# Attention by clusters with token mixing on one core: maxima over half the keys in single PSUM banks, weighted sums in runs of three units

## The chip, the cores and the metric

The kernel runs on one core of one Trainium2 chip. The metric is device time in microseconds (us), lower is better. TensorE multiplies matrices and writes PSUM, which has eight banks of 512 fp32 columns; VectorE (DVE in the profile), ScalarE (ACT), GpSimd (POOL) and SyncE (SP, which issues DMAs) work beside it. Each engine takes its instructions in order and waits for the others by semaphores.

## The reference

There are 4 batches, 8 heads, 768 positions, 64 columns to a head and 16 clusters. Attention goes only between a query and the keys of the same cluster; a token mixing layer follows. Cut to what matters:

```python
q_assign = np.argmax(np.einsum('bhsd,hcd->bhsc', q_n, c_n), axis=-1)
k_assign = np.argmax(np.einsum('bhsd,hcd->bhsc', k_n, c_n), axis=-1)
mask = q_assign[:, :, :, None] == k_assign[:, :, None, :]
scores = scale * np.matmul(q, k.transpose(0, 1, 3, 2))
scores = np.where(mask, scores, -1000000000.0)
scores = scores - np.max(scores, axis=-1, keepdims=True)
attn = np.exp(scores)
attn = attn / (np.sum(attn, axis=-1, keepdims=True) + 1e-09)
x = np.matmul(attn, v)          # heads side by side: 4 x 768 x 512
theta = x @ w_theta
y = w_tok_r @ (x * np.cos(theta)) + w_tok_i @ (x * np.sin(theta))
u = x + y
out = u + np.maximum(u @ w_ch, 0.0)
```

## The kernel before

Two heads of one batch make a **pair**; there are 16 pairs, and the two heads of one lie in partitions 0 to 63 and 64 to 127. The keys of a pair are cut into six tiles of 128 and the queries into two halves `a` of 384, so a pair has 12 **units** (`NU`), one for each half and tile of keys `i`, and the attention part has 192 (`NUT`).

In unit `u` the program issues, in this order:

- `scores(u)` (L335): four products for both heads, eight matmuls with 64 rows each into two PSUM banks of the pool `ps` (tiles `sc`). The last of the four, `mk` by `mq`, adds the mask and the negative row maximum. ScalarE takes the exponentials into a tile `at` (six buffers), and POOL adds them up by threes into `acc`.
- `row_max(u + LEAD)` (L304), in odd units only: the maxima of a tile of 128 queries over all 768 keys. Eight matmuls fill two tiles `m` of two banks each, one for each head, from the pool `ps0`, whose two buffers are four banks; then VectorE reduces 768 columns at a time into `nm`, with the sign turned.
- `weighted` (L387), in even units, for two units at a time, three and four units behind the scores: `at` by the values `vt`, matmuls with 128 rows, into the one bank `av`.
- whatever the table `todo` holds for that unit: the small pieces.

The small pieces of TensorE are `lg` (products with the cluster centres), `lt` (their transposes), `ot` (transposes of the one-hot assignments, twice a pair), `mt` (transpose of the maxima in `shift_row`, twice a pair) and `sm` (column sums of `acc` in `sums`). Behind `lt` VectorE finds the cluster of each query and key in steps of their own units: `mxl` and `eq` (L244, L246), the product with `wc` and the maximum `rr` (L250, L252), and `ohp` (L254). `A_UNITS`, `HI_UNITS`, `LO_UNITS`, `SUMS` and `NORM` say in which unit each step of a pair stands; a pair is prepared two pairs, 24 units, ahead of its scores. `shift_row` sends the transposed maxima by ScalarE and two DMAs into a row of `mq`, where `scores` reads them.

Besides, 14 blocks of weights are turned from 64-bit to 32-bit numbers and split. Block `x` starts at unit 13x; it has two VectorE instructions at 13x+4 (L128, L130, behind a ScalarE instruction, L127), two at 13x+8 (L133, L135), and a ScalarE copy and a POOL subtraction at 13x+11.

The order within an engine is fixed: `in_order` ties each instruction to the one in front of it on its engine, in the order in which the program issues them. A step that waits therefore holds up all that stands behind it on its engine. Tiles of a pool go round its buffers in turn, and a new tile waits until the old one's readers are done. Ahead of unit 0, the units from -LEAD on hold only maxima, pieces of the first pairs and two filling matmuls each (`WARM`). After the last unit the PSUM pools are closed and the token mixing part follows; its order is left to the scheduler, and the change does not touch it.

Of the kernel before, what the change touches and what calls it, by code (L numbers as in the profile page):

```python
# [9 lines left out]
F32 = mybir.dt.float32  # L10
# [4 lines left out]
ALU = mybir.AluOpType  # L15
AX = mybir.AxisListType
PSUM = bass.MemoryType.PSUM

BIG = float(2.0 ** 60)
N_M = 2  # L20
N_AV = 1
LEAD = 11
PW = 256
TAIL = 2
WARM = 2
SUMS = (5, 6, 8, 10, 12)
NORM = (14, 16)
TERMS = 3
EARLY = 3
LAG = 3  # L30
NAT = 6
AHEAD = 2
INV_2PI = float(1.0 / (2.0 * math.pi))
# [8 lines left out]
def kernel(  # L42
# [19 lines left out]
    nc = tc.nc  # L62
    B, H, D, S = qT.shape
    P = 128
    NP = H // 2
    NT = S // P
# [3 lines left out]
    HS = S // 2  # L70
# [7 lines left out]
    identf = cpool.tile([P, P], F32, name="identf")  # L78
# [83 lines left out]
    actx = ExitStack()  # L162

    ps0 = actx.enter_context(tc.tile_pool(name="ps0", bufs=N_M, space=PSUM))
    ps = actx.enter_context(tc.tile_pool(name="ps", bufs=8 - 2 * N_M - N_AV, space=PSUM))
    ps_av = actx.enter_context(tc.tile_pool(name="ps_av", bufs=N_AV, space=PSUM))
    pe = actx.enter_context(tc.tile_pool(name="pe", bufs=1))
    NPAIR = B * NP
# [1 line left out]
    for x in range(3):  # L170
        x = (NPAIR + x) % 3
# [4 lines left out]
    p2 = actx.enter_context(tc.tile_pool(name="p2", bufs=2))  # L176
    p1 = actx.enter_context(tc.tile_pool(name="p1", bufs=1))

    def bank(name, pool=None):
        return (pool or ps).tile([P, 512], F32, tag="bank", name=name)  # L180
# [28 lines left out]
    def f(ap):  # L209
        return ap.bitcast(F32)  # L210
# [78 lines left out]
    NH = NT // 2  # L289

    def split_u(u):
        pi, x = divmod(u, NU)
        return (pi,) + divmod(x, NT)

    def heads(*products):

        for n, (outs, stat, cols, mov, over) in enumerate(products):
            for j in range(2):
                r = slice(64 * j, 64 * j + 64)
                nc.tensor.matmul(  # L300
                    outs[j], lhsT=stat[r, cols], rhs=mov[r, over],
                    start=(n == 0), stop=(n == len(products) - 1))

    def row_max(u):  # L304


        pi, a, i = split_u(u)
        s = st[pi]
        if i == 0:
            s["nm", a] = p2.tile([P, 2, NH], F32, tag="nm", name=f"nm{u}")  # L310
        t = a * NH + i // 2
        m = [ps0.tile([P, 2, 512], F32, tag="m", name=f"m{u}_{j}") for j in range(2)]
        q = slice(t * P, (t + 1) * P)
        for c in range(2):
            k = slice(c * HS, (c + 1) * HS)
            outs = [m[j][:, c, 0:HS] for j in range(2)]
            heads((outs, s["hq"], q, s["hk"], k), (outs, s["mq"], q, s["mk"], k))
        for j in range(2):
            nc.vector.tensor_reduce(  # L319
                out=s["nm", a][:, j, i // 2:i // 2 + 1], in_=m[j][:, :, 0:HS], op=ALU.max, axis=AX.XY,  # L320
                negate=True)

    def shift_row(pi, a):

        s = st[pi]
        mt = bank(f"mt{pi}{a}")[0:NT, 0:P]
        nc.tensor.transpose(out=mt, in_=s["nm", a].rearrange("p j t -> p (j t)"), identity=identf)
        mr = p2.tile([NT, P], F32R, tag="mr", name=f"mr{pi}{a}")
        nc.scalar.copy(out=mr, in_=mt)
        for j in range(2):  # L330
            nc.sync.dma_start(
                out=f(s["mq"][64 * j + 32:64 * j + 33, a * HS:(a + 1) * HS]).rearrange("o (t n) -> o t n", n=P),
                in_=f(mr[j * NH:(j + 1) * NH]))
# [18 lines left out]
    def sums(pi):  # L352

        s = st[pi]
        sm = bank(f"sm{pi}")[:, 0:HS]
        for x in range(NT // TERMS):
            for j in range(2):
                for a in range(2):
                    g = 2 * j + a
                    nc.tensor.matmul(  # L360
                        sm[32 * g:32 * g + 32], lhsT=ecol, rhs=s["acc", a, x][:, j],
                        start=(x == 0), stop=(x == NT // TERMS - 1))
        se = p2.tile([P, HS], F32, tag="se", name=f"se{pi}", bufs=1)

        if pi < NPAIR - 1:
            nc.scalar.activation(out=se, in_=sm, func=AF.Identity, bias=eps)
        else:
            last_sum[0] = nc.vector.tensor_scalar_add(se, sm, 1e-9)
        yield

        sd = [dram.tile([4, HS], F32, tag=f"sd{x}", name=f"sd{x}{pi}", bufs=2) for x in range(2)]
        over = [x.rearrange("g (r n) -> (g r) n", r=32) for x in sd]
        nc.sync.dma_start(out=sd[0], in_=se.rearrange("(g r) n -> g r n", r=32)[:, 0])
        yield
        sq = p2.tile([P, 4 * HS // P], F32, tag="sq", name=f"sq{pi}")
        nc.sync.dma_start(out=sq, in_=over[0])
        yield
        nc.vector.reciprocal(out=sq, in_=sq)
        nc.sync.dma_start(out=over[1], in_=sq)
        yield  # L380
        s["rb"] = p1.tile([P, 2, HS], F32, tag="rb", name=f"rb{pi}")
        for j in range(2):
            last_load[0] = nc.sync.dma_start(
                out=s["rb"][64 * j:64 * j + 64],
                in_=sd[1][2 * j:2 * j + 2].unsqueeze(0).broadcast_to([64, 2, HS]))

    def weighted(u):  # L387
        pi, a, i = split_u(u)
        s = st[pi]
        if i == 0:  # L390
            s["av"] = ps_av.tile([P, 512], F32, tag="av", name=f"av{u}")[:, 0:HS]
        for j in range(2):
            nc.tensor.matmul(  # L393
                s["av"][64 * j:64 * j + 64], lhsT=s["vt"][:, i, j, :], rhs=s["at", a, i][:, j],
                start=(i == 0), stop=(i == NT - 1))
        if i == NT - 1:
            if a == 0:
                s["xt"] = p2.tile([P, 2, HS], F32, tag="xt", name=f"xt{pi}")
            nc.scalar.copy(out=s["xt"][:, a], in_=s["av"])

    def normalise(pi):
        b, p = divmod(pi, NP)
        s = st.pop(pi)

        (nc.gpsimd if pi < NPAIR - 2 else nc.vector).tensor_tensor(
            out=s["xt"], in0=s["xt"], in1=s["rb"], op=ALU.mult)
        yield
        nc.sync.dma_start(out=xT_d[b][:, p], in_=s["xt"].rearrange("p a s -> p (a s)"))
# [14 lines left out]
    NUT = NPAIR * NU  # L423
    todo = {}

    def at_unit(u, fn, *a):
        todo.setdefault(u, []).append((fn, a))

    def stages(units, gen):

        for u in units:
            at_unit(u, lambda: next(gen, None))
        at_unit(units[-1] + 1, run, gen)
# [15 lines left out]
                tail[ins.engine] = ins.name  # L449


    A_UNITS = (-2, 1, 3, 4, 6, 9, 11)
    HI_UNITS = dict(q=0, k=2)
    LO_UNITS = dict(q=2, k=4)
    W_UNITS = (4, 8, 11)
    W_EVERY = 13
    def prepare(pi, gen):
        u = NU * (pi - 2)
        stages([u + k for k in A_UNITS[1 if pi == 1 else 0:]], gen)
        for n in "qk":  # L460
            at_unit(u + HI_UNITS[n], part_hi, pi, n)
            at_unit(u + LO_UNITS[n], part_lo, pi, n, nc.gpsimd)

# [13 lines left out]
    for pi in range(NPAIR):  # L477
        u = NU * pi
        if pi > 0:
            prepare(pi, g1 if pi == 1 else assign(pi))  # L480
            at_unit(u - NU + 7, load_v, pi)
        for a in range(2):
            at_unit(u + a * NT - LEAD + NT, shift_row, pi, a)
        stages([u + NU + k for k in SUMS], sums(pi))
        stages([u + NU + k for k in NORM], normalise(pi))
    for x, gen in enumerate(early_weights()):
        u = W_EVERY * x
# [2 lines left out]

    idle = ps_av.tile([P, 512], F32, tag="av", name="idle")
    u = -LEAD
    while u < NUT + LAG or todo:
        start = len(nc.cur_bb.bb.instructions)
        if 0 <= u < NUT:
            scores(u)
        if u % 2 and u + LEAD < NUT:
            row_max(u + LEAD)
        for _ in range(WARM if u < 0 else 0):
            nc.tensor.matmul(idle[:, 0:P], lhsT=identb, rhs=identb, start=True, stop=True)  # L500
        if (u - LAG) % 2 and 0 <= u - LAG < NUT:
            weighted(u - LAG - 1)
            weighted(u - LAG)
        for x in sorted(x for x in todo if x <= u):
            for fn, a in todo.pop(x):
                fn(*a)
        in_order(start)
        u += 1
# [209 lines left out]
    u = None  # L718
    for part in range(S // PW):
# [4 lines left out]
        u = add_y(B - 1, part * PW, (part + 1) * PW)  # L724
# [53 lines left out]
```

## Time and profile before

| | us |
|---|---|
| median of 3 runs (lowest, highest) | 861.87 (858.85, 863.61) |
| the profiled execution, its own time | 864.6 |
| its span, first to last instruction | 862.8 |
| TensorE busy | 824.7 (96%) |
| VectorE busy | 466.8 (54%) |
| ScalarE busy | 402.5 (47%) |
| POOL busy | 470.6 (55%) |

Busy time of TensorE is modelled at the ends of its matmuls, and two matmuls that run side by side on 64 rows each count once; the distance from one start to the next says more than the length of one. A group's row gives: line, engine, operation, what it writes and reads, count, then busy time in us and the mean in ns of one, then the idle time of the engine just ahead of such instructions and what ended it. In a timeline row stand the start and the length in us, and at its end, in brackets, the idle time ahead of it. In a row of a stretch stand its ends and length, then busy time and count of TensorE, its weight loads, VectorE, ScalarE and POOL, then the granted TensorE clock (1.00 is full), the DMA share and GB/s.

### The profile page before, as it was taken

To read this page: it belongs to the slowest core of one execution; us is meant where nothing else is said; L and a number is where in the kernel's file an instruction comes from. 1 tells how busy PE (TensorE), PEld (TensorE's weight loads), DVE (VectorE), ACT (ScalarE), POOL (GpSimd) and SP (SyncE) were. 2 spreads that over 40 slices of the span, in tenths; PEclk is the share of its full clock that TensorE was granted. 3 is DMA by queue.
4 is the path that set the end of the run, shared out by engine and by line. 5 is a ranking of instruction groups with operands and counts; after the bars stand their busy time and mean duration, and the time that the engine had idled before them with its cause. 6 is when DMAs were issued, how large, how long until landed. Compare 5 with 4: busy or idle time off the path is not lost.

```text
span 862.8 us, 14648 instructions
## 1 busy us (share of the span) xinstructions
PE 824.7 (96%) x5863; PEld 599.2 (69%) x5863; DVE 466.8 (54%) x642; ACT 402.5 (47%) x802; POOL 470.6 (55%) x295
## 2 busy tenths in 40 slices
PE   5899899999999999999999989799999999999998
PEld 2655566565656555555666458589888988899998
DVE  4576576665775686477665188744423442343222
ACT  3246555565656555545655556432333333333220
POOL 3067668767887687677776636735122512251231
PEclk9699999999999999999999999899999999999999
DMA  2211222323223322213331152201200120010001
GB/s 94 65 53 45 88 86 65 128 87 101 80 88 111 112 76 93 81 53 102 99 119 57 56 178 98 73 1 50 98 2 1 50 98 1 1 49 26 1 13 63
DMA packets 27190, 59.09 MB, mean 68 GB/s; under 512 B 7793, under 2 KB 12657, under 8 KB 26737
## 3 DMA queue, kind: packets, MB, share of 16 engines
q1 hardware_dynamic: 26976, 57.75, 21.0%
q8 instruction: 46, 0.75, 0.4%
q10 hardware_dynamic: 144, 0.39, 0.1%
q14 instruction: 24, 0.19, 0.1%
HBM read 45.25 MB, written 12.78 MB: 67 GB/s over the span
## 4 chain that ended last, share of the span: by engine, by line
PE 77%; DVE 14%; DMA 4%; issue 2%; ACT 2%; POOL 1%; SPq 0%; ACTq 0%; DVEq 0%; POOLq 0%
PE y L648 21%; PE sc L300 16%; PE av L393 12%; PE m L300 7%; PE tp L581 6%; PE cy L671 4%; DVE nm L319 4%; PE cp L671 2%; DMA rawq<-in_qT_dram 2%; PE lg L232 2%; PE sm L360 2%; PE ot L262 1%; DVE w L130 1%; DVE w L135 1%; DVE eq L250 1%
## 5 line engine op out<-in xcount | busy, mean ns | idle before, releaser
L319 DVE TENSOR_REDUCE nm<-m 128x1 f32<-128x768 f32 x192 | 174.6, 950 | 145.5 <-PE m L300 145.5
L344 ACT ACTIVATE at<-sc 128x384 f32<-128x384 f32 x384 | 167.3, 489 | 122.8 <-PE sc L300 118.1
L350 POOL TENSOR_TENSOR acc<-at,at 128x768 f32<-128x768 f32 x64 | 120.7, 1886 | 99.7 <-ACT at L344 99.6
L393 PE MATMUL av<-at,vt 128*64 128x384 f32 x768 | 145.8, 501 | 0.0
L350 POOL TENSOR_TENSOR acc<-acc,at 128x768 f32<-128x768 f32 x64 | 123.1, 1923 | 28.9 <-ACT at L344 27.7
L602 POOL TENSOR_TENSOR zlc<-ab,zhc 128x512 fp32r<-128x512 f32 x24 | 31.9, 1330 | 170.8 <-ACT zhc L600 169.5
L300 PEld LDWEIGHTS sc<-hq,hk 64*128 64x128 f32 x384 | 41.4, 185 | 88.1 <-ACT at L344 60.9
L300 PE MATMUL sc<-hq,hk 64*128 64x384 f32 x384 | 92.4, 442 | 2.4 <-ACT at L344 2.4
L393 PEld LDWEIGHTS av<-at,vt 128*64 128x64 f32 x768 | 46.9, 137 | 59.4 <-issue 54.7
L300 PE MATMUL m<-hk,hq 64*128 64x384 f32 x384 | 76.1, 355 | 9.1 <-DVE nm L319 9.0
L300 PE MATMUL m<-mk,mq 64*128 64x384 f32 x384 | 73.5, 352 | 0.4 <-ACT mk L266 0.4
L300 PE MATMUL sc<-lq,hk 64*128 64x384 f32 x384 | 71.7, 340 | 0.0
L300 PE MATMUL sc<-mq,mk 64*128 64x384 f32 x384 | 70.8, 338 | 0.0
L300 PE MATMUL sc<-hq,lk 64*128 64x384 f32 x384 | 70.7, 338 | 0.0
L585 DVE TENSOR_SCALAR kk<-tp 128x512 int32<-128x512 f32 x24 | 16.5, 689 | 98.9 <-PE tp L581 98.9
L662 POOL TENSOR_TENSOR ul<-xT,uh 128x384 fp32r<-128x384 f32 (+1 forms) x36 | 33.9, 965 | 42.5 <-ACT uh L661 35.8
L576 ACT COPY xn<-xp 128x512 f32<-128x512 f32 x24 | 14.0, 585 | 88.6 <-PE xp L574 88.6
L648 PE MATMUL y<-wr_hi,zhc 128*128 128x512 f32 (+1 forms) x216 | 52.9, 320 | 1.8 <-ACT zhc L600 1.8
L300 PEld LDWEIGHTS m<-hk,hq 64*128 64x128 f32 x384 | 43.0, 193 | 15.4 <-DVE nm L319 15.0
L648 PE MATMUL y<-wr_hi,zlc 128*128 128x512 f32 (+1 forms) x216 | 52.9, 321 | 0.0
L648 PE MATMUL y<-wr_lo,zhc 128*128 128x512 f32 (+1 forms) x216 | 52.7, 320 | 0.0
L648 PE MATMUL y<-wi_hi,zhs 128*128 128x512 f32 (+1 forms) x216 | 52.5, 319 | 0.0
(143 smaller groups left out, 1641.0 us busy)
## 6 DMA issues: line engine op xcount, KB each, us to landing
rawq<-in_qT_dram SPq DMA_DIRECT2D x16, 384.0 KB
vt<-in_v_dram SPq DMA_DIRECT2D x16, 384.0 KB
rb<-sd SPq DMA_DIRECT2D x32, 192.0 KB
xT_d<-xt SPq DMA_DIRECT2D x16, 384.0 KB
rawk<-in_kT_dram SPq DMA_DIRECT2D x15, 384.0 KB
xT<-xT_d SPq DMA_DIRECT2D x3, 1536.0 KB
out_dram<-ot SPq DMA_DIRECT2D x24, 192.0 KB
w<-in_wrT_dram SPq DMA_DIRECT2D x3, 768.0 KB
```

Of the source, the lines that this page charges most:

```text
L232: nc.tensor.matmul(lg[32 * g:32 * g + 32], lhsT=cb[:, p, :, :], rhs=raws[n][:, a * HS:(a + 1) * HS], start=True, stop=True)
L300: nc.tensor.matmul(outs[j], lhsT=stat[r, cols], rhs=mov[r, over], start=(n == 0), stop=(n == len(products) - 1))
L319: nc.vector.tensor_reduce(out=s["nm", a][:, j, i // 2:i // 2 + 1], in_=m[j][:, :, 0:HS], op=ALU.max, axis=AX.XY, negate=True)
L344: last_exp[0] = nc.scalar.activation(out=at[:, j], in_=sc[j], func=AF.Exp, scale=SCALE)
L350: last_acc[0] = nc.gpsimd.tensor_tensor(out=s["acc", a, x], in0=prev, in1=at, op=ALU.add)
L360: nc.tensor.matmul(sm[32 * g:32 * g + 32], lhsT=ecol, rhs=s["acc", a, x][:, j], start=(x == 0), stop=(x == NT // TERMS - 1))
L393: nc.tensor.matmul(s["av"][64 * j:64 * j + 64], lhsT=s["vt"][:, i, j, :], rhs=s["at", a, i][:, j], start=(i == 0), stop=(i == NT - 1))
L581: nc.tensor.matmul(tp, lhsT=xx[:, c, :], rhs=w_th[c][k], start=(n == 0), stop=(n == 3 * NCT - 1))
L602: nc.gpsimd.tensor_tensor(out=zl, in0=tr, in1=zh.bitcast(F32), op=ALU.subtract)
L648: nc.tensor.matmul(y_at(b, d, c0, c1), lhsT=zz[:, d * P:(d + 1) * P], rhs=ww[:, c0:c1], start=first and lead, stop=last, skip_group_check= ...
L662: nc.gpsimd.tensor_tensor(out=ul[:, d, :], in0=x, in1=uh[:, d, :].bitcast(F32), op=ALU.subtract)
L671: nc.tensor.matmul(cp, lhsT=w_c[d][k][:, e * P:(e + 1) * P], rhs=uu[:, d, :], start=(n == 0), stop=(n == 3 * NCT - 1), skip_group_check=True)
```

## The change

- `row_max` runs in every unit, over half of the keys (384) at a time: four matmuls into two single banks, one for each head, out of three (`N_M` = 3, and a tile `m` is now one bank); VectorE reduces 384 columns at a time. `nm` holds both halves, and `shift_row` first takes the lesser of the two (the sign is turned) with a new VectorE instruction.
- The pool `ps` of the scores and small pieces has four banks instead of three.
- The maxima run 9 units ahead of the scores instead of 11.
- `weighted` comes in every third unit, for three units at a time, three to five units behind.
- All small pieces of TensorE stand in units 2, 5, 8 and 11 of 12, behind the weighted sums; the steps of the assignment, the splits of q and k, the sums and the normalisation move accordingly.

```diff
-N_M = 2
+N_M = 3
 N_AV = 1
-LEAD = 11
+LEAD = 9
...
-SUMS = (5, 6, 8, 10, 12)
-NORM = (14, 16)
+SUMS = (2, 3, 5, 7, 9)
+NORM = (11, 13)
 TERMS = 3
 EARLY = 3
-LAG = 3
+RUN = 3
...
-    ps = actx.enter_context(tc.tile_pool(name="ps", bufs=8 - 2 * N_M - N_AV, space=PSUM))
+    ps = actx.enter_context(tc.tile_pool(name="ps", bufs=8 - N_M - N_AV, space=PSUM))
...
         if i == 0:
-            s["nm", a] = p2.tile([P, 2, NH], F32, tag="nm", name=f"nm{u}")
-        t = a * NH + i // 2
-        m = [ps0.tile([P, 2, 512], F32, tag="m", name=f"m{u}_{j}") for j in range(2)]
-        q = slice(t * P, (t + 1) * P)
-        for c in range(2):
-            k = slice(c * HS, (c + 1) * HS)
-            outs = [m[j][:, c, 0:HS] for j in range(2)]
-            heads((outs, s["hq"], q, s["hk"], k), (outs, s["mq"], q, s["mk"], k))
+            s["nm", a] = p2.tile([P, 2, 2, NH], F32, tag="nm", name=f"nm{u}")
+        t, c = divmod(i, 2)
+        q0, k = (a * NH + t) * P, slice(c * HS, (c + 1) * HS)
+        m = [ps0.tile([P, 512], F32, tag="m", name=f"m{u}_{j}")[:, 0:HS] for j in range(2)]
+        q = slice(q0, q0 + P)
+        heads((m, s["hq"], q, s["hk"], k), (m, s["mq"], q, s["mk"], k))
         for j in range(2):
             nc.vector.tensor_reduce(
-                out=s["nm", a][:, j, i // 2:i // 2 + 1], in_=m[j][:, :, 0:HS], op=ALU.max, axis=AX.XY,
-                negate=True)
+                out=s["nm", a][:, c, j, t:t + 1], in_=m[j], op=ALU.max, axis=AX.X, negate=True)
...
+        nm = s["nm", a]
+        nc.vector.tensor_tensor(out=nm[:, 0], in0=nm[:, 0], in1=nm[:, 1], op=ALU.min)
         mt = bank(f"mt{pi}{a}")[0:NT, 0:P]
-        nc.tensor.transpose(out=mt, in_=s["nm", a].rearrange("p j t -> p (j t)"), identity=identf)
+        nc.tensor.transpose(out=mt, in_=nm[:, 0].rearrange("p j t -> p (j t)"), identity=identf)
...
-    A_UNITS = (-2, 1, 3, 4, 6, 9, 11)
-    HI_UNITS = dict(q=0, k=2)
-    LO_UNITS = dict(q=2, k=4)
+    A_UNITS = (-2, 2, 5, 6, 7, 8, 11)
+    HI_UNITS = dict(q=3, k=4)
+    LO_UNITS = dict(q=4, k=6)
...
-            at_unit(u + a * NT - LEAD + NT, shift_row, pi, a)
+            at_unit(u + a * NT - LEAD + NT - 1, shift_row, pi, a)
...
-    while u < NUT + LAG or todo:
+    while u < NUT + RUN or todo:
         start = len(nc.cur_bb.bb.instructions)
         if 0 <= u < NUT:
             scores(u)
-        if u % 2 and u + LEAD < NUT:
+        if u + LEAD < NUT:
             row_max(u + LEAD)
...
-        if (u - LAG) % 2 and 0 <= u - LAG < NUT:
-            weighted(u - LAG - 1)
-            weighted(u - LAG)
+        if (u + 1) % RUN == 0 and RUN <= u + 1 - RUN <= NUT:
+            for x in range(u + 1 - 2 * RUN, u + 1 - RUN):
+                weighted(x)
```

## The prediction

> **What bounds the kernel now.** I read the page's busy shares first, then the groups by shape, then the timeline of TensorE around single units.
>
> ```profile
> PE 824.7 (96%) x5863; PEld 599.2 (69%) x5863; DVE 466.8 (54%) x642; ACT 402.5 (47%) x802; POOL 470.6 (55%) x295
> ```
>
> TensorE bounds. The profiled execution took 864.6 us, 2.7 above the median of 861.87; I sum against it and take the 2.7 off at the end. The change lies in the attention part, whose first scores start at 34.36 us (row below, at the start) and last at 493.84: 191 units in 459.5 us, 28.9 us for the 12 of a pair.
>
> ```profile
> 304.11 0.44 PE L300 MATMUL sc<-hq,hk 64*128 64x384 f32 x2
> 304.39 0.34 PE L300 MATMUL sc<-lq,hk 64*128 64x384 f32 x2
> ...
> 304.91 0.33 PE L300 MATMUL m<-hk,hq 64*128 64x384 f32 x2
> ...
> 305.43 0.34 PE L300 MATMUL m<-mk,mq 64*128 64x384 f32 x2
> 305.70 0.55 PE L241 MATMUL lt<-identf,lgs 128*128 128x128 f32 x3
> ...
> 307.15 1.51 PE L393 MATMUL av<-at,vt 128*64 128x384 f32 x8
> 308.59 0.45 PE L300 MATMUL sc<-hq,hk 64*128 64x384 f32 x2
> ...
> 493.84 0.44 PE L300 MATMUL sc<-hq,hk 64*128 64x384 f32 x2
> ...
> 494.74 2.80 PE L393 MATMUL av<-at,vt 128*64 128x384 f32 x16
> ```
>
> The reader is to see the pitch, start to start. A slot of two heads' products costs 0.174 us (304.91 to 305.43 is three slots). The slot in front of a piece with 128 rows costs 0.27 (305.43 to 305.70), 0.10 more; the first slot behind one costs 0.28 (304.11 to 304.39), 0.11 more. A weighted run of two units takes 1.44 to the next score; its four slots are 1.29 (2.80 less 1.51), so it has 0.15 of its own at its ends.
>
> ```profile
> L319 DVE TENSOR_REDUCE nm<-m 128x1 f32<-128x768 f32 x192 | 174.6, 950 | 145.5 <-PE m L300 145.5
> ...
> L350 POOL TENSOR_TENSOR acc<-acc,at 128x768 f32<-128x768 f32 x64 | 123.1, 1923 | 28.9 <-ACT at L344 27.7
> ...
> L300 PE MATMUL sc<-hq,hk 64*128 64x384 f32 x384 | 92.4, 442 | 2.4 <-ACT at L344 2.4
> ...
> L300 PE MATMUL m<-hk,hq 64*128 64x384 f32 x384 | 76.1, 355 | 9.1 <-DVE nm L319 9.0
> ...
> L254 DVE TENSOR_TENSOR ohp<-wc,rr 128x384 bf16<-128x384 bf16 x16 | 19.9, 1244 | 0.0
> ...
> L250 DVE TENSOR_TENSOR eq<-eq,wc 128x384 bf16<-128x384 bf16 x16 | 18.1, 1133 | 0.5
> ...
> L232 PE MATMUL lg<-rawq,cb 128*32 128x384 f32 x64 | 16.6, 558 | 4.2 <-ACT at L344 3.6 <-DVE cb L206 0.6
> ...
> L135 DVE SCALAR_TENSOR_TENSOR w<-w,w 128x512 int32<-128x512 int32 x8 | 13.3, 1664 | 0.3
> ...
> L130 DVE TENSOR_SCALAR w<-w 128x512 int32<-128x512 int32 x8 | 11.0, 1371 | 0.3
> ...
> L135 DVE SCALAR_TENSOR_TENSOR w<-w,w 128x768 int32<-128x768 int32 x6 | 10.3, 1716 | 0.2
> ...
> L133 DVE SCALAR_TENSOR_TENSOR w<-w,w 128x768 int32<-128x768 int32 x6 | 9.8, 1627 | 0.0
> ...
> L128 DVE TENSOR_SCALAR w<-w 128x512 f32<-128x512 f32 x8 | 8.9, 1110 | 7.2 <-ACT w L127 7.2
> ...
> L252 DVE TENSOR_REDUCE rr<-eq 128x24 bf16<-128x384 bf16 x16 | 8.9, 553 | 0.6
> L244 DVE TENSOR_REDUCE mxl<-lt 128x24 f32<-128x384 f32 x16 | 8.8, 549 | 3.1 <-PE lt L241 3.1
> ...
> L133 DVE SCALAR_TENSOR_TENSOR w<-w,w 128x512 int32<-128x512 int32 x8 | 5.7, 717 | 0.0
> ...
> L128 DVE TENSOR_SCALAR w<-w 128x768 f32<-128x768 f32 x6 | 4.3, 717 | 6.8 <-ACT w L127 6.8
> ...
> L130 DVE TENSOR_SCALAR w<-w 128x768 int32<-128x768 int32 x6 | 3.4, 560 | 0.2
> ```
>
> **The change, part by part.**
>
> *Fewer switches (gain).* Before, every unit ends in a piece with 128 rows: the even ones in a weighted run, the odd ones in small pieces (lg, lt, sm, mt, ot at units 1, 3, 5, 7, 9, 11 of 12). After, all of them stand in units 2, 5, 8, 11 behind the run of three. 32 of 96 runs go: 32 x (0.10 + 0.11 + 0.15) = 11.5 us. 96 groups of small pieces lose their own way in and out: 96 x 0.2 = 19.2. Sum -31.
>
> *Old waits (gain).* TensorE's idle rows are 9.1 (maxima, waiting for reductions), 4.2 (lg), 2.4 (scores, waiting for a bank): 15.7, some 3 of it before the first score, and two spells of half clock of 1.7 each hang on the 9.1 (below). The scores get a fourth bank, lg comes 4 units after its loads instead of 3, so both go. I take -15 and book all new waits anew.
>
> *Start (gain).*
>
> ```profile
> 13.53 0.69 PE L300 MATMUL m<-hk,hq 64*128 64x384 f32 x2
> ...
> 22.60 0.36 DVE L250 TENSOR_TENSOR eq<-eq,wc 128x384 bf16<-128x384 bf16 x1
> ...
> 25.19 0.55 DVE L254 TENSOR_TENSOR ohp<-wc,rr 128x384 bf16<-128x384 bf16 x1
> ...
> 29.95 1.82 DVE L319 TENSOR_REDUCE nm<-m 128x1 f32<-128x768 f32 x2 [1.42 <-PE m L300]
> ...
> 34.36 0.69 PE L300 MATMUL sc<-hq,hk 64*128 64x384 f32 x2
> ```
>
> Six tiles of maxima take 20.8 us, TensorE and VectorE by turns. Nine halves over three banks overlap in part: about 1.45 each and 2 for the assignment, 15; three units' maxima (1 us) move into the run. -5.
>
> *Reductions.* No row shows one element out of 384. Bounds: half of 950 (475) and the 549 of L244, which reads 384 from PSUM. I take 0.55, next start after 0.47 (two of 950 take 1.82, so 0.08 overlaps). [...]
>
> *Where the reductions now stand (loss).* With three single banks, the second head's maxima of a unit need the bank of the first head's reduction of the unit before. Two units in three are now light: 0.70 of scores and 0.35 of maxima, 1.05. Maxima at t; their second slot starts at t+0.17 and lasts 0.34, so the reduction runs t+0.54 to t+1.09; the next maxima want t+1.05 and start at about 1.14: 0.1 x 64 runs = +6. So there is no room for anything between the reductions of two light units, and VectorE takes them in program order. Before, the four banks were asked for again only after two units, 4.8 us.
>
> *Assignment.* mult and rr stand behind the reductions of unit 6, ohp behind those of 7. From the first score of unit 6: maxima 6 at 0.80; its reductions 1.34 to 2.36; mult 2.28 to 3.41; rr to 3.99; reductions of 7, ready at 2.45, run 3.91 to 4.46 and 4.93; ohp to 6.1. Unit 8's maxima want 2.98 and get the bank at 4.51: 1.5 us, and 0.1 more because the heads start apart. The reductions of 8 end at 7.0, the new min at 7.2 (nearest small rows 0.2; at worst it waits for a POOL addition, 1.9), and mt, wanted at 7.15, takes another 0.1. 1.8 x 14 pairs = +25.
>
> *Weight conversion* x has instructions on VectorE at units 13x+4 (L128, L130, behind ACT) and 13x+8 (L133, L135). Behind the first light unit of a run they hold up the third unit's maxima in full: reductions end at t+1.53, then 1.63 + 1.72, so the next reduction ends at 5.35 where 2.16 was wanted, 3.2; L128 and L130 (0.72 + 0.56) start behind ACT's part at t+2.05, 1.7. In units 5 to 7 they push the assignment: behind rr at 3.99 another 1.11 + 1.37 moves unit 8's maxima from 4.51 to 7.0, 2.5. In front of a weighted run its 2.1 us hide most: 1.63 + 1.72 in unit 1 let the min of unit 2 end at t+6.0 where mt wants 5.0, 1.0. So, over x = 0 to 13: 1.3, 2.3, 2.5, 2.5, 0, 1.7, 0, 0, 1.7, 0, 0, 2.8, 1.3, 2.3 = 18; and 0.2, 2.3, 0, 0, 3.2, 1.0, 0, 3.2, 1.5, 3.1, 2.4, 2.4, 0.2, 2.3 = 22. A second wait in one run finds VectorE caught up, so a fifth off: +32. Ends: 12 and 50.
>
> *Clock.*
>
> ```profile
> 281.00 1.98 DVE L250 TENSOR_TENSOR eq<-eq,wc 128x384 bf16<-128x384 bf16 x1
> ...
> 283.48 1.81 DVE L319 TENSOR_REDUCE nm<-m 128x1 f32<-128x768 f32 x2
> ...
> 284.48 0.44 PE L300 MATMUL m<-hk,hq 64*128 64x384 f32 x1 [1.03 <-DVE nm L319]
> ...
> 285.34 0.44 PE L300 MATMUL m<-hk,hq 64*128 64x384 f32 x1 [0.42 <-DVE nm L319]
> ...
> 286.83 1.80 SPq L331 DMA_DIRECT2D mq<-mr  x2
> ```
>
> ```profile
> 283.13:286.54 3.41, 1.95 (x15) 1.01 (x11) 3.41 (x4) 0.87 (x2) 3.41 (x3) 1.00 0.23 87
> 286.54:289.95 3.41, 3.41 (x16) 1.75 (x16) 2.02 (x3) 1.12 (x3) 2.78 (x2) 0.50 0.04 9
> ```
>
> Here is the coming wait in the old trace, a late mult in front of reductions: TensorE idles 1.03 + 0.42 and the next 3.41 us run at clock 0.50, 1.7 us lost. I book 6 of these, half of the 12 longest waits: +10. [...]
>
> *At no cost.* hq, hk at 3, 4 and lq, lk at 4, 6: ACT and POOL have slack in the heavy unit, and rawq is loaded 5 units ahead of its cast instead of 2. sums starts 3 units earlier; its four DMAs keep their spacing on SP, and POOL's last addition is three units old by then. mt's copy and two DMAs (issued 1.80 long) have 6.2 us to the scores that need them; were landing to take over 4, the scores would wait. The 6 at buffers suffice, as the run stands behind the scores of the unit that reads last.
>
> **Sum.** 864.6 - 31 - 15 - 5 + 6 + 25 + 32 + 10 = 886.6; less 2.7: 884. New waits of 45 us (67 booked: 25 + 32 + 10) would just pay back the gains.
>
> **Rivals.**
> - *Faster: VectorE is quick enough for three banks.* mult has run in 0.36 and ohp in 0.55 (start-up, POOL idle) against means of 1.13 and 1.24; they wait for a POOL instruction to end. At those, the assignment costs 0.8 x 14 = 11, conversions in proportion 12, no clock lost: 840. Against: POOL's additions of 1.9 stand in the same light units. It decides below 40 us of new waits (857). 0.14.
> - *No change: waits partly covered*, 40 to 53 us of them: 857 to 870. 0.20, half of it within 0.5%.
> - *More clock lost:* 19 spells instead of 6, 32 us: 906. For: the one row above; against: a wait cut by the 3.41 us grid. 0.16.
> - *The change does not save its switches:* a piece behind the run costs as much as one behind maxima, 19 back: 903. For: no row shows a piece behind a run. Against: the rows at 304.11 and 305.70 charge the change between 64 and 128 rows, and pieces and runs both have 128. 0.05.
>
> **Numbers.** The forecast (870 to 896) gets 0.45. Half a per cent, 857.6 to 866.2, is what a measurement of this kernel can tell from no change. Faster 0.14, same 0.10, slower 0.76. The range 856 to 907 leaves out most of the first rival and the upper end of the third.
>
> **What will show it.** Right: idle ahead of m on TensorE, put down to the reductions, grows from 9 to 60 us and more; first slots at 0.28 fall to a third; reductions of 0.55; VectorE's other instructions stand in front of each long wait; lg's and the scores' idle vanishes; first score near 29 us. Wrong: that idle under 35 us, or the period of a pair under 28.

## The result and the profile after

| | before | after |
|---|---|---|
| median of the runs on one chip, us | 862.74 | 909.92 |
| ratio, with its 95% interval | 1 | 1.0545 (1.0493 to 1.0597) |
| span of the profiled execution, us | 862.8 | 908.6 |
| first score to last, us | 460.1 | 507.5 |
| TensorE busy in that stretch, us | 447.1 | 448.4 |

The change makes the kernel 47 us slower. Of two kernels below (the maxima alone with `mt` one unit earlier, and the conversions moved alone) the execution that was profiled ran far slower than the others as a whole, 4323 and 1814 us; their times are those of the other executions, and their idle times are not known.

Three rows of the page after: TensorE's busy time, its 40 slices, and the clock that it was granted in them.

```profile
PE 827.8 (91%) x5859; PEld 617.4 (68%) x5859; DVE 500.3 (55%) x866; ACT 397.6 (44%) x802; POOL 468.4 (52%) x295
...
PE   5998978979898889797798998979999999999998
...
PEclk9997989999999999898999999989999999999999
```

TensorE is as busy as before (824.7), in a span 45.8 us longer. But for two at the beginning of the token mixing part (slices 25 and 27) and one at the end, which the row of the kernel before has too, the holes (7 and 8) lie in the first 24 slices, which are the attention part; the clock dips in some of the same slices.

The groups of instructions after, with idle time ahead of each and what ended it:

```profile
L316 DVE TENSOR_REDUCE nm<-m 128x1 f32<-128x384 f32 x384 | 195.6, 551 | 145.7 <-PE m L300 139.2
L300 PE MATMUL m<-hk,hq 64*128 64x384 f32 x384 | 105.9, 389 | 43.5 <-DVE nm L316 43.5
L300 PE MATMUL sc<-hq,hk 64*128 64x384 f32 x384 | 91.3, 389 | 3.0 <-DVE eq L246 3.0
L250 DVE TENSOR_TENSOR eq<-eq,wc 128x384 bf16<-128x384 bf16 x16 | 13.7, 858 | 0.0
L254 DVE TENSOR_TENSOR ohp<-wc,rr 128x384 bf16<-128x384 bf16 x16 | 10.1, 634 | 0.0
L325 PE MATMUL mt<-identf,nm 128*6 128x128 f32 x32 | 9.2, 287 | 13.4 <-DVE nm L323 11.8 <-ACT xt L397 0.6
L232 PE MATMUL lg<-rawq,cb 128*32 128x384 f32 x64 | 15.3, 558 | 0.5 <-DVE cb L206 0.5
```

The idle time ahead of the maxima's products has gone from 9.1 to 43.5 us, and `mt` now waits 13.4; both wait for VectorE. A reduction of 384 columns takes 0.551 us. The idle time of `lg` has gone. The multiply and the compare of the assignment are quicker than before (858 and 634 ns for 1133 and 1244).

The whole attention stretch, before and then after (ends, length, busy time and count of TensorE, its weight loads, VectorE, ScalarE and POOL, granted clock, DMA share, GB/s):

```profile
34.36:494.47 460.11, 447.13 (x3605) 268.43 (x3605) 286.97 (x323) 264.18 (x558) 338.68 (x183) 0.99 0.27 84
```

```profile
31.99:539.47 507.48, 448.44 (x3609) 287.59 (x3609) 319.65 (x540) 259.02 (x558) 339.85 (x182) 0.94 0.24 77
```

Length less TensorE's busy time is its idle time: 13.0 us before, 59.0 after, 46 more. Busy time stayed as it was, though the change cuts switches, and the granted clock fell from 0.99 to 0.94; the last part works out how the two come to the same sum. The first score comes 2.4 us earlier, and what follows the attention is as long as before.

One of the long waits, in the timeline after:

```profile
77.14 0.35 PE L300 MATMUL m<-hk,hq 64*128 64x384 f32 x2
77.25 1.82 POOL L348 TENSOR_TENSOR acc<-acc,at 128x768 f32<-128x768 f32 x1
...
77.51 1.85 DVE L128 TENSOR_SCALAR w<-w 128x512 f32<-128x512 f32 x1
...
79.05 1.98 POOL L286 TENSOR_TENSOR lk<-rawk,hk 128x768 fp32r<-128x768 f32 x1
79.40 1.91 DVE L130 TENSOR_SCALAR w<-w 128x512 int32<-128x512 int32 x1
...
81.23 1.01 DVE L316 TENSOR_REDUCE nm<-m 128x1 f32<-128x384 f32 x2
...
81.83 0.68 PE L300 MATMUL m<-hk,hq 64*128 64x384 f32 x1 [3.12 <-DVE nm L316]
...
85.23 4.11 PE L391 MATMUL av<-at,vt 128*64 128x384 f32 x12
```

The maxima of 77.14 were ready for reduction by 77.7, but two conversion instructions stand in front of the reductions on VectorE, and each of them ends 0.3 us behind a POOL instruction that was running (79.36 behind 79.07, 81.31 behind 81.03). The reductions start at 81.23, and the next maxima have waited 3.12 us. The weighted run at 85.23 then takes 4.11 us, where one at full clock takes 2.16 (the row at 73.15 further down). This wait is no exception: TensorE's 32 waits of more than 0.6 us in the attention part are 55.8 us in all; in 24 of them, 48.8 us, conversion instructions stand on VectorE in front of the instruction that is awaited, and in 7 more, 5.7 us, other instructions of the assignment (multiply and `rr`).

Three of the stretches with the low clock, first the one behind this wait:

```profile
80.54:90.78 10.24, 8.77 (x38) 4.77 (x40) 6.33 (x12) 1.95 (x5) 4.44 (x3) 0.50 0.16 41
118.08:124.91 6.83, 5.48 (x20) 2.18 (x21) 4.01 (x8) 0.40 (x2) 2.42 (x2) 0.50 0.24 61
377.50:387.74 10.24, 8.37 (x36) 4.36 (x36) 6.73 (x12) 1.55 (x5) 4.84 (x3) 0.50 0.14 40
```

The clock stays low for up to 10.24 us. In the attention part there are 10 such spells with 58.0 us in all, in which TensorE was busy for 49.2. Inside a spell a slot of the scores takes 0.32 us (starts at 82.32, 82.64 and 82.96) instead of 0.174 and a run 4.11 instead of 2.16, so nearly half of these 49.2 us, some 24, went to the clock (an estimate from these rows).

The kernel before has two spells of 3.41 us in its attention part and the end of a longer one, which lasts from 23.71 to 40.78 us and so reaches past the first score (ends, length, TensorE's busy time and count, clock, DMA share, GB/s):

```profile
34.36:40.78 6.42, 6.16 (x34) 0.50 0.16 63
```

Together 13.2 us, busy for 13.0, of which some 6 went to the clock. In the changed kernel that spell around the first score is gone.

### The profile page after: what moved, and what is told of

Same layout as the page of the kernel before. It is cut to its first block, busy times and chain, and to the rows that moved or that the text cites. A ratio compares the mean times of both kernels' runs of the same rounds, so it can differ in the third digit from the quotient of the medians.

```text
span 908.6 us, 14888 instructions
## 1 busy us (share of the span) xinstructions
PE 827.8 (91%) x5859; PEld 617.4 (68%) x5859; DVE 500.3 (55%) x866; ACT 397.6 (44%) x802; POOL 468.4 (52%) x295
## 4 chain that ended last, share of the span: by engine, by line
PE 74%; DVE 20%; issue 2%; ACT 2%; DMA 1%; SPq 0%; POOL 0%; DVEq 0%; ACTq 0%
PE y L646 20%; PE av L391 13%; PE sc L300 12%; PE m L300 8%; PE tp L579 6%; DVE nm L316 5%; PE cy L669 4%; PE cp L669 2%; PE sm L358 2%; DVE w L130 2%; DVE w L128 2%; DVE w L135 2%; PE lg L232 2%; DVE w L133 2%; PE ot L262 1%
## 5 line engine op out<-in xcount | busy, mean ns | idle before, releaser
L316 DVE TENSOR_REDUCE nm<-m 128x1 f32<-128x384 f32 x384 | 195.6, 551 | 145.7 <-PE m L300 139.2
L300 PE MATMUL m<-hk,hq 64*128 64x384 f32 x384 | 105.9, 389 | 43.5 <-DVE nm L316 43.5
L300 PEld LDWEIGHTS m<-hk,hq 64*128 64x128 f32 x384 | 62.4, 198 | 64.6 <-DVE nm L316 54.3
L300 PE MATMUL m<-mk,mq 64*128 64x384 f32 x384 | 100.3, 378 | 0.4 <-ACT mk L266 0.4
L300 PE MATMUL sc<-lq,hk 64*128 64x384 f32 x384 | 81.7, 348 | 0.0
L300 PE MATMUL sc<-mq,mk 64*128 64x384 f32 x384 | 80.6, 345 | 0.0
L300 PE MATMUL sc<-hq,lk 64*128 64x384 f32 x384 | 80.0, 344 | 0.0
L300 PEld LDWEIGHTS sc<-hq,hk 64*128 64x128 f32 x384 | 52.2, 194 | 25.6 <-ACT mr L327 9.6
L397 ACT COPY xt<-av 128x384 f32<-128x384 f32 x32 | 15.3, 479 | 92.6 <-PE av L391 92.6
L300 PEld LDWEIGHTS m<-mk,mq 64*128 64x128 f32 x384 | 54.4, 202 | 0.8 <-ACT mk L266 0.8
```

The costliest lines, as they stand in the source:

```text
L300: nc.tensor.matmul(outs[j], lhsT=stat[r, cols], rhs=mov[r, over], start=(n == 0), stop=(n == len(products) - 1))
L316: nc.vector.tensor_reduce(out=s["nm", a][:, c, j, t:t + 1], in_=m[j], op=ALU.max, axis=AX.X, negate=True)
```

## The experiments

The theory after the result (A): VectorE has time enough; what costs is that its other instructions stand between the reductions of light units, where the three banks leave no slack. Against it stood that halves in three single banks are dear wherever the rest stands, and that it is VectorE's sum of work or the lost clock by itself that binds. Each expectation says what its letters stand for. Times are medians; the kernel before gave 859 to 862 beside them.

### Each half of the change alone

The runs of three and the pieces behind them, with the maxima as before:

```diff
-N_M = 3; LEAD = 9          # three single banks
+N_M = 2; LEAD = 11         # two double banks, whole rows, odd units
```

> Runs of three and small pieces behind them as in the changed kernel, the maxima as before (768 keys, two tiles of two banks, odd units, 11 ahead, three banks for the scores). Theory A (place: other VectorE instructions between the reductions of light units hold up the maxima, the single banks give room for one unit only, and the idle time costs clock): the switches are saved (18 to 31 us), but maxima of units 3 and 5 now stand close and three score banks bind in light units, 855 to 880 us. Rival B (halves and single banks cost by themselves, in more reductions): the whole saving shows, 830 to 842.

Measured: 901.0, ratio 1.0447 (1.0387 to 1.0506). Both theories missed. Its groups (`sc` are the scores):

```profile
L300 PE MATMUL sc<-hq,hk 64*128 64x384 f32 x384 | 117.8, 416 | 36.7 <-ACT at L344 21.6 <-DVE eq L246 12.2
L262 PE MATMUL ot<-identb,ohp 128*128 128x128 bf16 x192 | 17.4, 232 | 15.5 <-DVE ohp L254 15.0 <-ACT mr L329 0.5
```

The wait has gone over to the scores. The double banks leave the scores three banks, which they share with the small pieces; two light units in a row fill them, and then they wait for exponentials and for `eq`, which frees the bank of `lt`. By this reading the runs need the fourth score bank, which only the maxima's change sets free, so that the two halves of the change belong together; no run gives these runs a fourth bank alone or moves VectorE's instructions here, so that is argued, not shown. `ot` waits too, 15.0 us, for `ohp` on VectorE.

The maxima by halves in three banks, with weighted pairs and pieces as before:

```diff
-RUN = 3                    # weighted runs and pieces in units 2, 5, 8, 11
+LAG = 3                    # weighted pairs in even units, pieces in odd ones
```

> Maxima over half the keys in single banks, lead of 9, four score banks as in the changed kernel; weighted sums, small pieces and VectorE's steps as before. Theory A: every unit is 1.9 to 2.7 us long, so a VectorE instruction finds room: 853 to 868 us, TensorE's idle time ahead of m under 25 us. Rival B: 885 to 910, idle ahead of m over 40.

Measured: 942.98, ratio 1.0951 (1.0910 to 1.0992). It fits neither: the idle time is not where B puts it.

```profile
L300 PE MATMUL m<-hk,hq 64*128 64x384 f32 x384 | 83.0, 377 | 11.7 <-DVE nm L316 11.5
L325 PE MATMUL mt<-identf,nm 128*6 128x128 f32 x32 | 9.5, 297 | 60.2 <-DVE nm L323 60.2
```

`mt` stood in an odd unit right behind the last maxima, with no weighted run to cover the reductions and the minimum: 60.2 us of idle, made by the experiment. The next one puts it one unit earlier.

```diff
-at_unit(u + a * NT - LEAD + NT, shift_row, pi, a)
+at_unit(u + a * NT - LEAD + NT - 1, shift_row, pi, a)
```

> The kernel before with the maxima of the change alone (half the keys in every unit, three single banks, lead of 9), weighted sums and small pieces as before; unlike the run of the maxima alone, the transpose of the maxima stands one unit earlier, behind a pair of weighted sums that covers the last reductions and their minimum. A, in the run of the maxima alone it was the place of the transpose that cost (60 us of idle ahead of it), and halves in single banks cost nothing by themselves: 850 to 872, idle ahead of the transpose under 15 us. B, halves and three banks are slower than whole rows whatever stands behind them: 885 or more, with the idle time ahead of the maxima's products.

Measured: 903.4, ratio 1.0498 (1.0444 to 1.0552), some 40 us better, but still in B's range; where its idle time lies is not known. That left two readings: halves are dear, or VectorE's other instructions, still placed as before, now stand in the wrong units. The last run of this group tells them apart: the same kernel with those instructions in the even units, in which the weighted pairs stand. The edit takes TensorE's `lg`, `lt` and `ot` into even units with them, and spaces the weight blocks 12 units apart instead of 13.

```diff
-A_UNITS = (-2, 1, 3, 4, 6, 9, 11); W_UNITS = (4, 8, 11); W_EVERY = 13
+A_UNITS = (-7, -4, -2, 4, 6, 8, 8); W_UNITS = (4, 5, 11, 14); W_EVERY = 12   # and start at 12x + 9
```

> The kernel before with the maxima of the change alone (halves in every unit, three single banks, lead of 9, transpose behind a pair of weighted sums, which gave 904) and VectorE's other work moved into the even units, which have the weighted pairs: conversions 2 and 8, multiply and rr 4, compare 6, logits' maxima -2. A, halves in single banks cost nothing where VectorE's other instructions stand in units with weighted sums: 842 to 862, idle ahead of the maxima's products under 15 us. B, halves or three banks have a cost of their own: 880 or more, idle over 30 us with the instructions in the even units.

Measured: 848.08, ratio 0.9856 (0.9826 to 0.9885). That is A: the same work in another order is worth some 55 us, and halves in three single banks are then no slower than the kernel before; they are 1.4% faster. Its idle ahead of the maxima and its attention stretch:

```profile
L301 PE MATMUL m<-hk,hq 64*128 64x384 f32 x384 | 91.0, 368 | 8.2 <-DVE nm L317 8.2
```

```profile
36.74:479.84 443.10, 434.23 (x3606) 272.20 (x3606) 341.40 (x538) 253.25 (x556) 340.64 (x183) 1.00 0.27 88
```

The pieces that moved along are not what made the difference: TensorE's busy time here is what it was in the run of the maxima alone with its old order, 433 us, once the clock that was lost there is taken off (466.6 us at a mean clock of 0.93, of which some 66 at half clock; an estimate). What went is the idle time, 8.9 us here and 71.5 there, and the low clock.

### VectorE's other instructions: left out, or moved

The changed kernel without the four conversion instructions of each of the 14 weight blocks (the arithmetic on their bits is missing from the output):

```diff
+        if not arith:
+            yield
+            return w            # ahead of L128
```

> The changed kernel without VectorE's four conversion instructions for each of the 14 early weight blocks (so these weights are not the right numbers); all else the same. Theory A with the sizes of the prediction: the conversions' waits (32 us) and half of the clock lost go, 858 to 878 us, idle ahead of m near 25. Rival C (what is late is the assignment and the reductions themselves, conversions mostly fill gaps): 890 to 905.

Measured: 838.39, ratio 0.9736 (0.9695 to 0.9777). Its attention part:

```profile
32.55:467.85 435.30, 422.95 (x3609) 275.37 (x3609) 244.94 (x484) 258.29 (x558) 330.34 (x182) 1.00 0.28 90
```

TensorE's idle time is 12.4 us, and the mean clock of the stretch is 1.00. Without these 56 instructions 72 us are gone, more than any theory gave them. The same taken out of the kernel before:

> The kernel before without VectorE's four conversion instructions of each early weight block (the low bits of those weights are then missing from the output), as was done in the changed kernel, where it gave 72 us. A, in the kernel before these instructions lie beside other work all but a few: 848 to 857. B, the kernel before pays for them as well, so that the place of them would have been worth as much there: 800 to 840.

Measured: 846.02, ratio 0.9801 (0.9775 to 0.9827): 16 us, a little past the end of A. The kernel before pays something for them, the changed one four and a half times that. Its attention part:

```profile
35.20:477.00 441.80, 439.38 (x3606) 266.90 (x3605) 221.01 (x267) 264.57 (x558) 331.42 (x183) 0.99 0.27 88
```

Only 2.4 us of idle time are left in it. So this run also says how much the kernel before could gain by a better order, which was not run: with these instructions gone altogether it takes 846, and the changed kernel with all of them, in the next run, takes less.

Now the changed kernel with all its work, only in another order: multiply and `rr` in unit 2, compare in 5, conversions in 2 and 8, reciprocal in 8, all of them heavy units.

```diff
-SUMS = (2, 3, 5, 7, 9);  A_UNITS = (-2, 2, 5, 6, 7, 8, 11)
+SUMS = (2, 3, 5, 8, 9);  A_UNITS = (-7, -4, -1, 2, 5, 8, 8)
-W_UNITS = (4, 8, 11);  W_EVERY = 13
+W_UNITS = (4, 5, 11, 14);  W_EVERY = 12      # start at 12x + 9
         nc.scalar.activation(out=w, in_=high.bitcast(F32), func=AF.Abs)
+        yield
```

> The changed kernel with VectorE's other instructions moved to the heavy units, where the weighted run covers them: mult and rr in unit 2, ohp in 5, conversions in 2 and 8, the reciprocal in 8; the same work, three m banks, same runs. Theory A: TensorE's idle time ahead of m falls below 20 us, no spells of half clock after the start, 825 to 850 us. Rival B (halves and three banks) and a rival D (VectorE simply has too much to do): 885 or more, since nothing is taken away.

Measured: 837.68, ratio 0.9730 (0.9687 to 0.9772), and once more beside the last version:

> The version with both kinds moved once more, beside the one with the earlier start on the same chip: 837 to 840, 0.97 of the kernel before.

Measured: 833.57, ratio 0.9672 (0.9636 to 0.9708), a little quicker than expected. Its attention stretch, its group, and a heavy unit in its timeline:

```profile
37.12:465.87 428.75, 416.57 (x3599) 272.99 (x3598) 335.51 (x540) 254.73 (x556) 338.95 (x182) 1.00 0.27 91
```

```profile
L301 PE MATMUL m<-hk,hq 64*128 64x384 f32 x384 | 97.2, 372 | 12.0 <-DVE nm L317 12.0
```

```profile
70.90 3.21 DVE L317 TENSOR_REDUCE nm<-m 128x1 f32<-128x384 f32 x6 [0.71 <-PE m L301]
...
73.05 1.82 POOL L349 TENSOR_TENSOR acc<-at,at 128x768 f32<-128x768 f32 x1 [3.60 <-ACT at L343]
73.15 2.16 PE L392 MATMUL av<-at,vt 128*64 128x384 f32 x12
74.03 1.26 DVE L255 TENSOR_TENSOR ohp<-wc,rr 128x384 bf16<-128x384 bf16 x1
...
75.24 0.45 PE L301 MATMUL sc<-hq,hk 64*128 64x384 f32 x2
...
76.05 0.34 PE L301 MATMUL m<-hk,hq 64*128 64x384 f32 x2
```

VectorE's busy time in the attention part is even larger than in the changed kernel (335.5 for 319.7), and TensorE's idle time is 12.2 us for 59.0. The compare at 74.03 ends 0.4 us behind POOL's addition (75.29 behind 74.87) and takes twice its time, but TensorE is in the weighted run, and the maxima of 76.05 wait for nothing. Six reductions go back to back. This is A; neither halves, three banks nor VectorE's sum of work makes the change slow, since all three are still there. The edit again takes pieces of TensorE along: `lg`, `lt` and `ot` go from one heavy unit to another, and the two groups of `ot` come to stand in one unit.

Each kind moved alone, first the conversions:

> The changed kernel with only VectorE's two pairs of conversion instructions of the early weight blocks moved, to units 2 and 8 of a pair of heads; the assignments stay where the change puts them (multiply and rr in unit 6, compare in unit 7). Leaving the conversions out altogether gave 838, moving both kinds gave 838. A, it is where the conversions stand that costs, and the assignments cost little by themselves: 838 to 850, idle time ahead of the maxima's products under 20 us. B, the assignments cost the 25 us that the prediction booked, and only with nothing else of VectorE's work in the pair are they covered: 860 to 875, idle ahead of the maxima 30 to 40 us. C, neither alone helps: 895 or more.

Measured: 849.8, ratio 0.9877 (0.9827 to 0.9926), by the time as A; its idle time is not known. Then the assignments:

> The changed kernel with only the assignments moved (multiply and rr in unit 2, compare in unit 5, as in the run with both moved); the conversions stay at every 13th unit with steps 4 and 8 units later, so that they fall in light and heavy units by turns. A, the conversions are what costs, and the assignments little: 880 to 905, idle ahead of the maxima still over 40 us and some 8 half-clock spells. B, the assignments are a third or more of it: 850 to 870. C, two things of VectorE in one unit are what hurts, so that taking away either kind clears it: 835 to 850.

Measured: 895.39, ratio 1.0400 (1.0339 to 1.0462), again A, with 37.5 us of idle ahead of the maxima where A said over 40. So the conversions' place is worth 60 us and the assignments' 15; both together gave 72 and 76. They add up. Some 3 of the 15 are not waits: `ot`, whose two groups now share a unit, keeps TensorE busy for 15.2 us instead of 18.4.

### POOL's part

The changed kernel without the second of POOL's two additions in each run (a third of the exponentials is then missing from the sums):

```diff
-        if y > 0:
+        if y == 1:
             prev = ...
```

> The changed kernel without GpSimd's second addition in each run of three units (the third unit's exponentials are left out of the sums of rows). It asks whether VectorE's instructions wait for GpSimd's additions. A, they do, and that lengthens VectorE's stalls: the conversions' instructions go from 1.2 to 1.4 us to about 1.0, and the time to 870 to 895. B, the wait is VectorE's own work and the two engines don't matter to each other: 905 to 912, with the same durations.

Measured: 881.14, ratio 1.0266 (1.0194 to 1.0339): 29 us less, as A. Two of the conversion's lines (count, then shortest, median and longest in ns), in the changed kernel and then without the addition; behind the semicolon stand the shapes:

```profile
L130 DVE TENSOR_SCALAR w<-w x14: 427/1907/2069, 45.3 to 505.9; 128x512 int32<-128x512 int32 x8, 128x768 int32<-128x768 int32 x6
...
L135 DVE SCALAR_TENSOR_TENSOR w<-w,w x14: 691/2190/2471, 55.9 to 515.2; 128x512 int32<-128x512 int32 x8, 128x768 int32<-128x768 int32 x6
```

```profile
L130 DVE TENSOR_SCALAR w<-w x14: 426/559/2039, 46.1 to 479.6; 128x512 int32<-128x512 int32 x8, 128x768 int32<-128x768 int32 x6
...
L135 DVE SCALAR_TENSOR_TENSOR w<-w,w x14: 691/825/2456, 56.3 to 488.9; 128x512 int32<-128x512 int32 x8, 128x768 int32<-128x768 int32 x6
```

The medians leap because such an instruction is either quick or held up: 9 of the 14 at L130 took over 1.9 us, and 3 without the addition. The mean of all 56 conversion instructions goes from 1.38 us (77.0 in all) to 1.04 (58.3), as A had it. Leaving out the addition also gives POOL less to do ahead of its other work; what that alone is worth was not run.

In the timeline of the changed kernel a POOL instruction was under way at the start of each of these 9 at L130 (six times an addition, three times a subtraction of L286), and each of them ended 0.28 to 0.42 us behind it. At the start of the 5 quick ones none was, and a POOL instruction that began beside a quick one did not hold it up: the one at 223.51, with an addition from 223.60 on, took 0.56. What makes the one engine wait for the other is not shown.

### A version with an earlier start

In the moved version the first score came at 37.1 us instead of 32.0, so the first two prepared pairs were put back nearly into the change's own order.

> The version with both kinds of VectorE's work moved, but the first two prepared pairs keep nearly the change's own order (pair 1: units as in the change; pair 2: load at unit -2, logits 0, transposes 1, multiply and rr 2, compare 5), since in that version the first score came at 37.1 us and in the changed kernel at 32.0. A, the start is earlier and nothing of it is given back: 832 to 835, first score at 32 to 33 us. B, the work held back from the start comes due in the first pairs and takes the gain: 837 to 842.

Measured: 835.92, ratio 0.9695 (0.9672 to 0.9719), beside 833.57 for the version without it; the intervals overlap. The first score came at 32.7 us, but no gain of the time can be measured. In either order the changed kernel is faster than the kernel before by 3%.

## Why the prediction was wrong

Forecast 884 (856 to 907), measured 909.9. The direction held, and so did the mechanism: VectorE's instructions between the reductions make TensorE wait, and the idle time ahead of `m` is charged to the reductions. Two sizes failed, the clock and the maxima of two heads that start apart. Term by term:

| term | booked, us | measured, us | from |
|---|---|---|---|
| TensorE's idle time in the attention part (new waits 25 + 32, less 12 old ones) | +45 | +46 | the two stretches |
| clock (10, less 3 for the old spells) | +7 | +18 | some 24 lost after, some 6 before |
| reductions between light units | +6 | about +15 (estimate) | TensorE's starts, below |
| switches | -31 | about -32 (estimate) | the rest of TensorE's busy time |
| start | -5 | -2.4 | first score 34.36, then 31.99 |

Booked together: +22. Measured from span to span: +45.8, of which idle time is 46, TensorE's busy time 1.3 (that is clock, reductions and switches together), the start -2.4 and the part behind the attention 0.8.

**Clock: the step that failed most, by 11 us.** It priced a spell at 1.7 us, one stretch of 3.41, and took 6. There were 10, and they lasted 3.4 to 10.2 us. Cut into stretches, the spell from 80.54 to 90.78 reads (ends, length, TensorE's busy time and count, clock, DMA share, GB/s):

```profile
80.54:83.95 3.41, 2.12 (x12) 0.50 0.00 0
83.95:87.37 3.42, 3.24 (x13) 0.50 0.26 40
87.37:90.78 3.41, 3.41 (x19) 0.50 0.22 82
```

The long wait that began it ends at 81.83, in the first of the three. In this trace all 10 spells end with a stretch in which TensorE is busy throughout, and those that are longer go through stretches with idle time in them (0.67 to 3.24 us busy); the stretch ahead of each of the 10 has 0.55 to 1.67 us of busy time, and no other stretch of the attention part at full clock has under 1.9. That is read from the trace and was not tested.

The prediction also passed over the long spell around the first score of the kernel before, 17.07 us, which showed that a spell can outlast one stretch; it even went on behind one in which TensorE was busy throughout (30.54 to 33.95, busy 3.41 us, with the clock at 0.50 in it and in the stretches on both sides). The rival with more lost clock (19 spells of 1.7, 32 us) was nearer to the sum, by another way: fewer and longer. Where only 8.9 to 12.4 us of idle time were left (the attention stretches above of the maxima moved, the moved version and the one without conversions), the mean clock was 1.00.

The waits ahead of the two short spells of the old trace were 1.59 + 0.43 us (ended at 53.53 and 54.40) and 1.03 + 0.42 us (ended at 284.48 and 285.34); behind each pair the clock was 0.50 for 3.41 us. How long a wait must be to cost clock is not shown.

**Reductions: the second step, short by some 9 us.** It booked 0.1 us a run, as a wait. In fact the second head's matmuls start late while the first head's run, so that the loss shows as busy time, and it is larger. In the moved version's trace, in the second light unit and in the heavy one, a pair of products is 0.55 long:

```profile
71.57 0.55 PE L301 MATMUL m<-mk,mq 64*128 64x384 f32 x2
...
72.67 0.56 PE L301 MATMUL m<-mk,mq 64*128 64x384 f32 x2
```

It is 0.34 with both heads together. From the scores at 70.70 to the run at 73.15 TensorE takes 2.45 us for slots that need 11 x 0.174 + 0.27 = 2.18, and is not idle. Worked out from all starts, the slots ahead of a run take 0.28 us too long in the median, in the changed kernel as in the moved version: some 18 us in 64 runs, against some 3 in the kernel before.

**Switches.** The booked -31 about held: what is left of TensorE's busy time when clock and late heads are taken off comes to -32. It is a remainder, and no run has the switches alone. The rival that denied those savings finds no support in the starts: a run's last slot takes 0.42 us in front of a piece and in front of a score alike, and that 0.10 is part of the 0.15 which the prediction left with each run.

**The idle time came out right by luck:** its two parts missed in opposite directions.

- *Assignment, +25.* Moving it brought 15 of time and 7.3 of idle (59.0 to 51.7), and without the conversions no more than 12.4 of idle are left for it. The step took the old means for `mult` and `ohp` (1.13 and 1.24) into the new place; there they took 0.86 and 0.63. That POOL was less often in an instruction beside them would explain it, but was not tested apart.
- *Conversions, +32.* The idle time that goes with them is 46.6 us (59.0 less 12.4 without them), most of the 13.4 ahead of `mt` among them (3.9 without them). Their whole price, clock included, is 72. The old durations explain a part of the miss only: L130 went from a median of 561 ns before to 1907, but L135 stayed at 2.2 us, and all 56 together went from 66.6 to 77.0 us. The prediction took a fifth off its sum of 40 for waits that overlap; whether that was the rest of the miss stays open.

**Right:** reductions of 0.55; the idle time of `lg` gone, and the part behind the attention unchanged to within 1 us. First slots of 0.28 did fall to a third of the units, the one behind each heavy unit: worked out from the starts in the moved version's trace, the median first slot is 0.17. Not as foreseen: the idle time ahead of `m` is 43.5, between the 60 that was to show the forecast right and the 35 that was to show it wrong, and the scores still wait 3.0 us, now for `eq`.

**The forecast's reason for the old waits, -15,** is half true: 12.2 us of idle remain in the moved version, 10.7 of them ahead of `m`, with the last conversion instruction (L135, there L136) in front of the reductions.

Left open: why the start gained 2.4 us and not 5. And the time of the halves alone with the old order (903.4) is explained only through the run that changed the order.

## What to carry to other kernels

When a change makes a resource tight (here the banks of the maxima, asked for again after one unit instead of two), look through everything that the releasing engine has in its queue between two releases, and move it behind a long stretch of other work: the same instructions in another order made the difference between 5% slower and 3% faster. Take a duration into a new place only after asking what ran beside it in the old one, since here the same instruction took 0.56 or 1.91 us by what POOL was doing. And count a wait on TensorE with the half clock that followed it here: with 46 us of new idle time came some 18 more.

## What the runs showed of the hardware

With a wait of 3.12 us came a clock of 0.50 for 10.24 us (80.54 to 90.78), longer than the 3.41 behind the waits of the old trace; it came back behind the first stretch of 3.41 us in which TensorE was not idle (87.37 to 90.78), though the long spell of the old trace went on behind such a stretch (30.54 to 33.95). Of the 14 instructions at L130, the 9 at whose start a POOL instruction was under way took over 1.9 us, the other 5 took 0.43 to 0.56; leaving out 64 of POOL's additions made that 3 of 14 and the kernel 29 us quicker. When the matmuls of two heads, which run side by side on 64 rows each, start 0.2 us apart, the loss (about 0.28 us a run) shows as busy time of TensorE and not as idle time.
